# Attention into a gated MLP on one core: another order for the first loads, and a last output piece in two parts

## The chip, the cores and the metric

The kernel runs on one core of a Trainium2 chip. The metric is the device time of one execution in microseconds; the profile's span, from the first to the last instruction, lies inside it. The engines are named as in the profile: PE (TensorE matmul), PEld (its weight loads), DVE (VectorE), ACT (ScalarE), POOL (GpSimd) and SP (SyncE, which issues most DMAs).

## The reference

Eight batches, 12 heads, 448 positions, head size 64, all float32. An attention whose softmax has one extra term in its denominator feeds a layer with a mish-gated hidden width:

```python
scores = (q @ k.T) / sqrt(64)
m = max(scores, axis=-1)
e = exp(scores - m)
attn = e / (sum(e) + exp(-m) + 1e-9)
x = (attn @ v), heads side by side        # 3584 x 768
h = x @ w_in                              # 3584 x 2048
g = h * tanh(softplus(h))
out = g @ w_out                           # 3584 x 768, float32
```

## The kernel before, in words

Work is cut into pairs of heads: 48 pairs, six to a batch, numbered through as p. A pair's q, k and v are loaded by `load_pair` (L118) as tiles of 112 partitions, each with 4 neighbouring positions of both heads, one DMA of 224 KB each, issued by SP in program order. `cast_pair` (L155) turns them into bf16: on GpSimd, except pair 0, whose q goes to VectorE and whose k goes to ScalarE. `transpose_pair` (L171) turns q and k by eight PE transposes into PSUM; for pair 0 q and k have a PSUM tile each, for the following pairs both share one. `evac_qk` (L199) brings them back to SBUF, q scaled by 1/8; for pair 0 ScalarE takes q and VectorE takes k.

`scores` (L244) does the matmuls of one of four steps of a pair into one of three PSUM tiles (`sc_tiles`), and VectorE's negated row maximum (L285). `exps` (L291) is ScalarE's exponential with its row sum (L298). `normalise` issues a DMA transpose of the exponentials on SP (L370), or `turn_on_pe` does part of it on PE (L381); `spread_rden` spreads the reciprocals over PSUM by matmuls (L341); `av_pair` multiplies by v (L407). `mm1_mish` does the first MLP product (L438) and mish on ScalarE (L444). `mm2_part` (L463) is the second product (L485), cut into small chunks that fill PE between attention steps. Its `evac` copies PSUM to an output tile on VectorE (L472), and `store_rows` (L448) issues the stores on SP (L456), two DMAs for 128 rows, because the rows of one tile belong to two of the interleaved position sets; the very last tile (group 3, tile 6) is stored in two column parts as these are ready. For its last 128 rows the first DMA has 16 rows and the second 112.

The order is written out by hand: `tc.manual_schedule()` keeps each engine's instructions in program order, and semaphores are set by the tiles that instructions read and write. Buffers: 3 for each loaded float32 tile, 4 for the bf16 q and k, 12 for the bf16 v. In the built program a load is also held until the one eight places before it on SP has landed.

The program begins like this (L535 on): three pairs are loaded, each as q, k, v; pairs 0 and 1 are cast and transposed, with pair 0's evacuation and its first three score steps after its own transposes; then pair 3 is loaded, pair 2 cast, three weight pieces are issued on GpSimd's queue (`load_w`), pair 4 is loaded. Then the first batch's six pairs follow in a loop of pairs and steps (the head); evacuation of pair 1 follows the first `exps`. After that come units of three pairs with the MLP work between them.

Of the kernel before, what the change touches and what calls it, by code (L numbers as in the profile page):

```python
# [10 lines left out]
BF16 = mybir.dt.bfloat16  # L11
AF = mybir.ActivationFunctionType
ALU = mybir.AluOpType
AX = mybir.AxisListType

UNIT_PAIRS = 3
# [3 lines left out]
def kernel(  # L20
# [9 lines left out]
    nc = tc.nc  # L30

    B, H, S, D = q.shape
# [3 lines left out]
    NT = 4  # L36
    SP_ = S // NT
# [9 lines left out]
    SCALE = 1.0 / float(D) ** 0.5  # L47
# [5 lines left out]
    def pool(name, bufs, space=None):  # L53
# [18 lines left out]
    sc_tiles = [  # L72
        psum.tile([128, 2, 512], FP32, tag=f"sc{i}", name=f"sc{i}") for i in range(3)
    ]
# [26 lines left out]
    loaded, casted, qkT, att, xT, o_sbs, stats = {}, {}, {}, {}, {}, {}, {}  # L101
# [3 lines left out]
    def flush_late():  # L105
        while late:
            late.popleft()()

    def mo_take():

        if not mo_free:
            flush_late()
        return mo_free.popleft()
# [1 line left out]
    spread_copy = {}  # L115


    def load_pair(p):  # L118
        if p >= N_PAIRS:
            return  # L120
        b, h0 = p // HP, (p % HP) * 2
        tiles = []
        for nm, src in (("q", q), ("k", k), ("v", v)):
            t = ld_pool.tile([SP_, 2, NT * D], FP32, tag=f"{nm}_f", name=f"{nm}_f")
            nc.sync.dma_start(  # L125
                out=t, in_=src[b, h0 : h0 + 2].rearrange("h (p t) d -> p h (t d)", t=NT)
            )
            tiles.append(t)
        loaded[p] = tiles


    def w_pieces():
# [16 lines left out]
    def load_w(n):  # L149
        for _ in range(min(n, len(pieces))):  # L150
            dst, src = pieces.popleft()
            nc.gpsimd.dma_start(out=dst, in_=src.rearrange("(a p) c -> p a c", p=128))


    def cast_pair(p):  # L155
        if p >= N_PAIRS:
            return
        q_f, k_f, v_f = loaded.pop(p)
        q_bf = bf_pool.tile([SP_, NT, 2, D], BF16, tag="q_bf", name="q_bf")
        k_bf = bf_pool.tile([SP_, NT, 2, D], BF16, tag="k_bf", name="k_bf")  # L160
        v_bf = bf_pool.tile([SP_, 2, NT * D], BF16, tag="v_bf", name="v_bf", bufs=12)
        by_t = "p h (t d) -> p t h d"
        cast_q, cast_k = nc.gpsimd.tensor_copy, nc.gpsimd.tensor_copy
        if p == 0:
            cast_q, cast_k = nc.vector.tensor_copy, nc.scalar.copy
        cast_q(out=q_bf, in_=q_f.rearrange(by_t, t=NT))  # L166
        cast_k(out=k_bf, in_=k_f.rearrange(by_t, t=NT))  # L167
        nc.gpsimd.tensor_copy(out=v_bf, in_=v_f)  # L168
        casted[p] = (q_bf, k_bf, v_bf)

    def transpose_pair(p, bank=None):  # L171
        if p >= N_PAIRS:
            return
        q_bf, k_bf, _ = casted[p]
        if bank is None:
            ps = mo_take()
            ps_k = mo_take() if p == 0 else ps
        else:
            ps, ps_k = sc_tiles[2 - bank][:, 0, :], sc_tiles[2 - bank][:, 1, :]
        by_s = [  # L180
            t[:, :].bitcast(BF16).rearrange("p (s n) -> p s n", s=2)[:, s, :]
            for s, t in enumerate((ps, ps_k))
        ]
        for s, src in enumerate((q_bf, k_bf)):
            for t in range(NT):
                nc.tensor.transpose(  # L186
                    by_s[s][:, t * SP_ : (t + 1) * SP_],
                    src[:, t].rearrange("p h d -> p (h d)"),
                    ident[:SP_, :SP_],
                )  # L190
        own = [] if bank is not None else [ps, ps_k] if p == 0 else [ps]
        qkT[p] = (by_s, own)

    def apart(later, *earlier):

        for e in earlier:
            tc.declare_no_dep(later.ins, e.ins, reason="they read different PSUM banks")

    def evac_qk(p, act=False):  # L199
        if p >= N_PAIRS:  # L200
            return
        (q_ps, k_ps), own = qkT[p]
        mo_free.extend(own)
        q_reads = []
        qd = q_diag[p % 3]
        kT = qk_pool.tile([128, S], BF16, tag="kT", name="kT")
        if p < DIAG_FROM:
            qT = qd.rearrange("d i h r -> d (i h r)")[:, 0:S]
            qkT[p] = (qT, kT)
            if act:  # L210
                nc.scalar.mul(qT, q_ps[:, 0:S], SCALE)
            else:
                q_reads.append(nc.vector.tensor_scalar(
                    out=qT, in0=q_ps[:, 0:S], scalar1=SCALE, scalar2=None, op0=ALU.mult
                ))
        else:
            qkT[p] = (qd, kT)
            if p < DIAG_FROM + 3:
                nc.vector.memset(qd[0:64, :, 1, :], 0.0)
                nc.vector.memset(qd[64:128, :, 0, :], 0.0)  # L220
            for h in range(2):
                rows = slice(64 * h, 64 * h + 64)
                q_reads.append(nc.vector.tensor_scalar(  # L223
                    out=qd[rows, :, h, :],
                    in0=q_ps[rows, 0:S].rearrange("d (i r) -> d i r", i=QB),
                    scalar1=SCALE, scalar2=None, op0=ALU.mult,
                ))
        if p == 0 or own and not act:
            nc.vector.tensor_copy(out=kT, in_=k_ps[:, 0:S])
        else:  # L230
            k_read = nc.scalar.copy(kT, k_ps[:, 0:S])  # L231
            if not own:
                apart(k_read, *q_reads)
# [3 lines left out]
    def scores_ahead(limit):  # L237

        while rg["next"] < limit and rg["used"] < len(sc_tiles):
            rg["used"] += 1  # L240
            scores(rg["next"])
            rg["next"] += 1
# [202 lines left out]
        if not spare:  # L445
            mo_free.append(h_ps)

    def store_rows(g, i, o_sb, cols):  # L448

        r = i * 128  # L450
        while r < (i + 1) * 128:
            seg = r // SP_
            n = min((i + 1) * 128, (seg + 1) * SP_) - r
            b, t, c0 = 2 * g + seg // NT, seg % NT, r % SP_
            rows = out[b * S : (b + 1) * S, :].rearrange("(c t) m -> t c m", t=NT)
            nc.sync.dma_start(  # L456
                out=rows[t, c0 : c0 + n, cols], in_=o_sb[r - i * 128 : r - i * 128 + n, cols]
            )
            r += n
# [3 lines left out]
    def mm2_part(g, i, q0, nq):  # L463

        cols, n_cols = slice(q0 * NQ, (q0 + nq) * NQ), nq * NQ
        st = {}

        def evac():
            if (g, i) not in o_sbs:
                o_sbs[g, i] = [o_pool.tile([128, d_model], FP32, tag="o_sb", name="o_sb"), 0]  # L470
            o_sb, have = o_sbs[g, i]
            nc.vector.tensor_copy(out=o_sb[:, cols], in_=st["o"][:, 0:n_cols])  # L472
            mo_free.append(st["o"])
            o_sbs[g, i][1] = have + nq
            if (g, i) == (B // 2 - 1, 6):
                store_rows(g, i, o_sb, cols)
            elif have + nq == 4:
                store_rows(g, i, o_sb, slice(0, d_model))

        def chunk(f0, f1):  # L480
            if f0 == 0:
                flush_late()
                st["o"] = mo_take()
            for ff in range(f0, f1):
                nc.tensor.matmul(  # L485
                    st["o"][:, 0:n_cols],
                    lhsT=gT[:, ff, i * 128 : (i + 1) * 128],
                    rhs=w_out_sb[:, ff, cols],
                    start=(ff == 0), stop=(ff == FF_T - 1),
                )  # L490
            if f1 == FF_T:
                late.append(evac)

        step = 2
        return [(lambda f0=f0: chunk(f0, f0 + step), nq) for f0 in range(0, FF_T, step)]
# [36 lines left out]
    TURN_BY_ACT = {(HEAD - 1, 3)}  # L532

    W_AT = ({1: 1, 5: 1, 9: 1}, {1: 1, 5: 1, 7: 1, 9: 1, 11: 1}, {1: 1, 3: 1, 5: 1, 7: 1})
    for p in range(UNIT_PAIRS):  # L535
        load_pair(p)
    for p in range(2):
        cast_pair(p)
        transpose_pair(p)
        if p == 0:  # L540
            evac_qk(p, act=True)
            scores_ahead(3)
    load_pair(3)
    cast_pair(2)
    load_w(3)
    load_pair(4)


# [35 lines left out]
    for u in range(UNITS_PER_B, N_UNITS + 2 * UNITS_PER_B):  # L584
# [10 lines left out]
        for n in range(steps):  # L595
            pi, s = divmod(n, STEPS)
            p, idx = p0 + pi, p0 * STEPS + n
            late_tp = u == UNITS_PER_B and n == STEPS
            if late_tp:
                transpose_pair(p0 + 2)  # L600
# [38 lines left out]
        for f in range(FF_U):  # L639
# [19 lines left out]
            if f in (3, FF_U - 1) and p0 >= LATE_DIV:  # L659
                p = todo[1 + f // (FF_U - 1)]  # L660
# [33 lines left out]
```

## Time and profile before

| what | value |
|---|---|
| median of 3 runs | 493.13 us (493.05 to 497.79) |
| the profiled execution, device time | 488.69 us |
| its span | 486.9 us |
| mean granted TensorE clock | 0.987 |
| PE busy | 453.3 us, 93% of the span |
| VectorE busy | 359.4 us, 74% |
| ScalarE busy | 345.4 us, 71% |
| GpSimd busy | 103.4 us, 21% |
| HBM read, written | 45.61 MB, 11.01 MB |

How to read it: in the page's picture of 40 slices PE is at nine tenths or more from the eleventh slice on, save for the last one. The chain of waits follows the work that ended last, backwards. A timeline row has start, duration, engine, line, operation, output and input tile, and the idle time before it with what ended it. [...] The profiled execution was quicker than any of the three timed runs, so the steps of a sum are held against the execution, and only their difference is set against the median.

### The profile page before, as it was taken

The page shows a single profiled execution, that of the slowest core. Times are in us where ns is not written, and L with a number is a line of the kernel's source. Part 1 is how long each engine was busy: PE and PEld are TensorE (multiplying, and loading weights), DVE is VectorE, ACT ScalarE, POOL GpSimd, SP SyncE. Part 2 cuts the span into 40 slices and gives each one's busy share as a digit, 9 for nine tenths or more (in the row PEclk, how much of TensorE's full clock was granted, in tenths as well). Part 3 has the DMA queues.
Part 4 walks back from the last instruction along what each step waited for, and adds up shares of the span by engine and source line. Part 5 has one row for each costly group of instructions (what it writes and reads, how often), then busy time and mean ns, then how long its engine had stood idle before and what let it go on. Part 6 is the DMA issues. An engine that isn't in the chain of part 4 may idle for free.

```text
span 486.9 us, 9223 instructions
## 1 busy us (share of the span) xinstructions
PE 453.3 (93%) x3219; PEld 258.4 (53%) x3219; DVE 359.4 (74%) x713; ACT 345.4 (71%) x905; POOL 103.4 (21%) x184
## 2 busy tenths in 40 slices
PE   4676896898999999999999999999999999999996
PEld 2344454554655565555555555555555555556563
DVE  4889738758889898889899888889898978520011
ACT  5998859677687887879687868788797968412300
POOL 4534535206013030403012120404040200000000
PEclk9999798999999999999999999999999999999999
DMA  8999999999998979799999998998979886761122
GB/s 233 221 235 206 265 197 241 145 185 246 143 220 224 204 195 197 230 194 258 164 247 174 221 209 190 223 199 223 199 236 164 210 152 142 146 146 31 36 59 72
DMA packets 204975, 91.08 MB, mean 187 GB/s; under 512 B 161792, under 2 KB 201472, under 8 KB 204928
## 3 DMA queue, kind: packets, MB, share of 16 engines
q1 hardware_dynamic: 197440, 84.20, 79.5%
q0 software_dynamic: 7488, 6.29, 9.0%
q8 instruction: 25, 0.41, 0.4%
q14 instruction: 22, 0.18, 0.1%
HBM read 45.61 MB, written 11.01 MB: 116 GB/s over the span
## 4 chain that ended last, share of the span: by engine, by line
PE 75%; ACT 11%; DVE 8%; DMA 2%; issue 2%; SPq 1%; POOL 0%; DVEq 0%; ACTq 0%
PE mo L438 26%; PE mo L485 24%; ACT en L298 9%; PE sc L264 7%; DVE negm L285 6%; PE sc L407 5%; PE sc L438 4%; PE sc L186 3%; PE mo L407 2%; DMA k_f<-in_k_dram 1%; PE mo L341 1%; PE sc L270 1%; DMA v_f<-in_v_dram 1%; SPq L125 1%; DVE eT L385 1%
## 5 line engine op out<-in xcount | busy, mean ns | idle before, releaser
L298 ACT ACTIVATE en<-sc,negm 128x448 bf16<-128x448 f32 x336 | 208.4, 641 | 22.6 <-DVE negm L285 20.7
L285 DVE TENSOR_REDUCE negm<-sc 128x2 f32<-128x896 f32 x192 | 183.0, 971 | 44.8 <-PE sc L264 28.2
L485 PE MATMUL mo<-w_out_sb,gT 128*128 128x384 bf16 (+1 forms) x1024 | 166.7, 306 | 0.0
L438 PE MATMUL mo<-xT,w_in_sb 128*128 128x448 bf16 x672 | 141.9, 353 | 0.5 <-DVE xT L417 0.3
L485 PEld LDWEIGHTS <-gT 128*128 128x128 bf16 x1024 | 96.3, 98 | 55.4 <-issue 1.3
L444 ACT ACTIVATE gT<-mo 128x448 bf16<-128x448 f32 x112 | 59.6, 543 | 83.0 <-PE mo L438 82.7
L438 PEld LDWEIGHTS <-w_in_sb 128*128 128x128 bf16 x768 | 72.7, 98 | 63.6 <-issue 3.3
L166 POOL CAST q_bf<-q_f 112x512 bf16<-112x512 f32 x47 | 29.3, 623 | 230.8 <-DMA q_f<-in_q_dram 208.0
L362 DVE TENSOR_SCALAR en<-en,rden 128x448 bf16<-128x448 bf16 x252 | 73.6, 365 | 0.8
L264 PE MATMUL sc<-kT,qd 128*128 128x448 bf16 x252 | 71.6, 354 | 0.0
L298 ACT ACTIVATION_READ_ACCUMULATOR en<-sc,negm 128x1 f32 x336 | 71.1, 212 | 0.0
L472 DVE COPY o_sb<-mo 128x384 f32<-128x384 f32 (+1 forms) x64 | 32.1, 501 | 48.3 <-PE mo L485 48.1
L264 PEld LDWEIGHTS <-qd 128*128 128x128 bf16 x252 | 24.6, 97 | 28.8 <-issue 12.9
L407 PE MATMUL sc<-eT,v_bf 112*64 112x448 bf16 x288 | 34.1, 357 | 2.1 <-ACT en L298 1.6
L223 DVE TENSOR_SCALAR qd<-sc 64x448 bf16<-64x448 bf16 x72 | 27.7, 385 | 7.5 <-PE sc L186 6.6
L407 PEld LDWEIGHTS <-v_bf 112*64 112x64 bf16 x384 | 20.9, 111 | 22.3 <-issue 15.6
L168 POOL CAST v_bf<-v_f 112x512 bf16<-112x512 f32 x48 | 29.9, 624 | 12.2 <-DMA v_f<-in_v_dram 11.5
L167 POOL CAST k_bf<-k_f 112x512 bf16<-112x512 f32 x47 | 29.1, 619 | 9.1 <-DMA k_f<-in_k_dram 8.0
L270 PE MATMUL sc<-kT,qd 64*128 64x448 bf16 x36 | 15.8, 457 | 7.7 <-ACT en L298 7.2
L186 PEld LDWEIGHTS <-q_bf 112*128 112x128 bf16 x192 | 14.3, 103 | 15.4 <-DVE q_bf L166 4.2
L231 ACT COPY kT<-sc 128x448 bf16<-128x448 bf16 x39 | 20.8, 534 | 0.6 <-PE sc L186 0.6
L438 PE MATMUL sc<-xT,w_in_sb 128*128 128x448 bf16 x96 | 20.8, 353 | 0.0
(53 smaller groups left out, 279.2 us busy)
## 6 DMA issues: line engine op xcount, KB each, us to landing
q_f<-in_q_dram SPq DMA_DIRECT2D x48, 224.0 KB, 5.3
k_f<-in_k_dram SPq DMA_DIRECT2D x48, 224.0 KB, 5.4
v_f<-in_v_dram SPq DMA_DIRECT2D x48, 224.0 KB, 5.5
w_in_sb<-in_moe_w_in_dram POOLq DMA_DIRECT2D x12, 256.0 KB, 7.3
w_out_sb<-in_moe_w_out_dram POOLq DMA_DIRECT2D x8, 384.0 KB, 7.4
out_dram<-o_sb SPq DMA_DIRECT2D x7, 336.0 KB, 3.5
out_dram<-o_sb SPq DMA_DIRECT2D x8, 288.0 KB, 5.0
out_dram<-o_sb SPq DMA_DIRECT2D x8, 240.0 KB, 3.5
```

The costliest lines, as they stand in the source:

```text
L166: cast_q(out=q_bf, in_=q_f.rearrange(by_t, t=NT))
L167: cast_k(out=k_bf, in_=k_f.rearrange(by_t, t=NT))
L168: nc.gpsimd.tensor_copy(out=v_bf, in_=v_f)
L264: nc.tensor.matmul(sc[:, bk, 0:S], lhsT=qT[:, i].rearrange("d h r -> d (h r)"), rhs=kT, start=True, stop=True,)
L285: nc.vector.tensor_reduce(out=negm, in_=sc[:, 0 : len(cols), 0:S], axis=AX.X, op=ALU.max, negate=True)
L298: e = nc.scalar.activation(out=st["en"][:, :, c, 0:SP_], in_=sc[:, bk, 0:S].rearrange("q (j c) -> q j c", j=NT), func=AF.Exp, bias=st["neg ...
L362: nc.vector.tensor_scalar(out=en[:, :, i, 0:SP_], in0=en[:, :, i, 0:SP_], scalar1=st["rden"][:, i : i + 1], scalar2=None, op0=ALU.mult,)
L407: nc.tensor.matmul(av[h * 64 : (h + 1) * 64, 0:S], lhsT=v_bf[:, h, j * D : (j + 1) * D], rhs=e_h, start=(j == 0), stop=(j == NT - 1),)
L438: nc.tensor.matmul(h_ps[:, 0:S], lhsT=w_in_sb[:, dm, ff * 128 : (ff + 1) * 128], rhs=xT[b][:, dm, :], start=(dm == 0), stop=(dm == DM_T - 1),)
L444: nc.scalar.activation(out=gT[:, ff, b % 2 * S : b % 2 * S + S], in_=h_ps[:, 0:S], func=AF.Mish)
L472: nc.vector.tensor_copy(out=o_sb[:, cols], in_=st["o"][:, 0:n_cols])
L485: nc.tensor.matmul(st["o"][:, 0:n_cols], lhsT=gT[:, ff, i * 128 : (i + 1) * 128], rhs=w_out_sb[:, ff, cols], start=(ff == 0), stop=(ff == ...
```

## The change

What it does, in four pieces:

- The first nine loads stand in another order on SP: k 0, q 0, q 1, k 1, v 0, q 2, k 2, v 1, v 2.
- Pair 0 is cast on VectorE alone: k first, then q in two halves (two of the four column blocks each). PE turns k first, then q, with the second half of q going to a free score tile, `sc_tiles[2]`. ScalarE evacuates k, VectorE evacuates q in two halves.
- The casts of v for pairs 0, 1 and 2 are their own function on GpSimd: v 0 after the casts of q and k of pair 1, v 1 and v 2 after those of pair 2.
- In the very last output piece (384 columns) VectorE copies the first 192 columns and ScalarE the other 192; of its two stores the one of 16 rows is issued on ScalarE's queue, the one of 112 rows stays on SP.

```diff
-    def load_pair(p):
+    def load_pair(p, names="qkv"):
...
-        for nm, src in (("q", q), ("k", k), ("v", v)):
+        for nm in names:
+            src = dict(q=q, k=k, v=v)[nm]
...
-    def cast_pair(p):
+    def cast_pair(p, with_v=True):
...
         if p == 0:
-            cast_q, cast_k = nc.vector.tensor_copy, nc.scalar.copy
-        cast_q(out=q_bf, in_=q_f.rearrange(by_t, t=NT))
-        cast_k(out=k_bf, in_=k_f.rearrange(by_t, t=NT))
-        nc.gpsimd.tensor_copy(out=v_bf, in_=v_f)
+            nc.vector.tensor_copy(out=k_bf, in_=k_t)
+            for half in (slice(0, NT // 2), slice(NT // 2, NT)):
+                nc.vector.tensor_copy(out=q_bf[:, half], in_=q_t[:, half])
+        else:
+            nc.gpsimd.tensor_copy(out=q_bf, in_=q_t)
+            nc.gpsimd.tensor_copy(out=k_bf, in_=k_t)
         casted[p] = (q_bf, k_bf, v_bf)
+        if with_v:
+            cast_v(p)
+
+    def cast_v(p):
+        nc.gpsimd.tensor_copy(out=casted[p][2], in_=loaded.pop(p)["v"])
...
-        for s, src in enumerate((q_bf, k_bf)):
+        by_2 = sc_tiles[2][:, 0, :].bitcast(BF16)
+        srcs = list(enumerate((q_bf, k_bf)))
+        for s, src in reversed(srcs) if p == 0 else srcs:
             for t in range(NT):
+                to = by_2 if p == 0 and s == 0 and t >= NT // 2 else by_s[s]
                 nc.tensor.transpose(
-                    by_s[s][:, t * SP_ : (t + 1) * SP_],
+                    to[:, t * SP_ : (t + 1) * SP_],
...
+            if p == 0:
+                nc.scalar.copy(kT, k_ps[:, 0:S])
+                by_2 = sc_tiles[2][:, 0, :].bitcast(BF16)
+                for ps, half in (q_ps, slice(0, S // 2)), (by_2, slice(S // 2, S)):
+                    nc.vector.tensor_scalar(
+                        out=qT[:, half], in0=ps[:, half], scalar1=SCALE, scalar2=None,
+                        op0=ALU.mult,
+                    )
+                return
...
-            nc.sync.dma_start(
+            (queue if queue is not None and n < SP_ else nc.sync).dma_start(
...
-            nc.vector.tensor_copy(out=o_sb[:, cols], in_=st["o"][:, 0:n_cols])
+            last = (g, i, have + nq) == (B // 2 - 1, 6, 4)
+            n_dve = n_cols // 2 if last else n_cols
+            nc.vector.tensor_copy(
+                out=o_sb[:, cols.start : cols.start + n_dve], in_=st["o"][:, 0:n_dve]
+            )
+            if last:
+                nc.scalar.copy(o_sb[:, cols.start + n_dve : cols.stop], st["o"][:, n_dve:n_cols])
...
-                store_rows(g, i, o_sb, cols)
+                store_rows(g, i, o_sb, cols, queue=nc.scalar if last else None)
...
-    for p in range(UNIT_PAIRS):
-        load_pair(p)
+    for p, names in (0, "kq"), (1, "qk"), (0, "v"), (2, "qk"), (1, "v"), (2, "v"):
+        load_pair(p, names)
     for p in range(2):
-        cast_pair(p)
+        cast_pair(p, with_v=False)
         transpose_pair(p)
         if p == 0:
-            evac_qk(p, act=True)
+            evac_qk(p)
             scores_ahead(3)
     load_pair(3)
-    cast_pair(2)
+    cast_v(0)
+    cast_pair(2, with_v=False)
+    cast_v(1)
+    cast_v(2)
```

More of the change, by code (lines that the diff above doesn't have):

```diff
@@ L121, in load_pair @@
         b, h0 = p // HP, (p % HP) * 2
-        tiles = []
-        for nm, src in (("q", q), ("k", k), ("v", v)):
+        for nm in names:
+            src = dict(q=q, k=k, v=v)[nm]
             t = ld_pool.tile([SP_, 2, NT * D], FP32, tag=f"{nm}_f", name=f"{nm}_f")
@@ L127, in load_pair @@
             )
-            tiles.append(t)
-        loaded[p] = tiles
+            loaded.setdefault(p, {})[nm] = t
     def w_pieces():
@@ L152, in load_w @@
             nc.gpsimd.dma_start(out=dst, in_=src.rearrange("(a p) c -> p a c", p=128))
-    def cast_pair(p):
+    def cast_pair(p, with_v=True):
         if p >= N_PAIRS:
             return
-        q_f, k_f, v_f = loaded.pop(p)
+        q_f, k_f, v_f = (loaded[p].get(nm) for nm in "qkv")
         q_bf = bf_pool.tile([SP_, NT, 2, D], BF16, tag="q_bf", name="q_bf")
@@ L162, in cast_pair @@
         by_t = "p h (t d) -> p t h d"
-        cast_q, cast_k = nc.gpsimd.tensor_copy, nc.gpsimd.tensor_copy
+        q_t, k_t = (t.rearrange(by_t, t=NT) for t in (q_f, k_f))
         if p == 0:
-            cast_q, cast_k = nc.vector.tensor_copy, nc.scalar.copy
-        cast_q(out=q_bf, in_=q_f.rearrange(by_t, t=NT))
-        cast_k(out=k_bf, in_=k_f.rearrange(by_t, t=NT))
-        nc.gpsimd.tensor_copy(out=v_bf, in_=v_f)
+            nc.vector.tensor_copy(out=k_bf, in_=k_t)
[4 more added lines that the diff above has]
+            nc.gpsimd.tensor_copy(out=k_bf, in_=k_t)
         casted[p] = (q_bf, k_bf, v_bf)
+        if with_v:
+            cast_v(p)
+    def cast_v(p):
+        nc.gpsimd.tensor_copy(out=casted[p][2], in_=loaded.pop(p)["v"])
     def transpose_pair(p, bank=None):
@@ L227, in evac_qk @@
                 ))
-        if p == 0 or own and not act:
+        if own and not act:
             nc.vector.tensor_copy(out=kT, in_=k_ps[:, 0:S])
@@ L446, in mm1_mish, with store_rows @@
             mo_free.append(h_ps)
-    def store_rows(g, i, o_sb, cols):
+    def store_rows(g, i, o_sb, cols, queue=None):
         r = i * 128
```

## The prediction

> **What bounds the kernel now.** I read four views: the page's head, the chain of waits, the timeline of the first 16 us, and the last 5 us. First the page:
>
> ```profile
> span 486.9 us, 9223 instructions
> PE 453.3 (93%) x3219; PEld 258.4 (53%) x3219; DVE 359.4 (74%) x713; ACT 345.4 (71%) x905; POOL 103.4 (21%) x184
> PE 75%; ACT 11%; DVE 8%; DMA 2%; issue 2%; SPq 1%; POOL 0%; DVEq 0%; ACTq 0%
> ```
>
> TensorE (PE) carries three quarters of the chain. The change touches none of that steady part: compared in the built programs, every engine's order is the same outside the first and last dozen instructions. So the question is how much earlier the steady part begins, and how much sooner the span closes after PE's last matmul. The chain of waits, from the start (start us, us, what):
>
> ```profile
> 2.67 5.62 DMA k_f<-in_k_dram
> 8.35 0.62 POOL k_bf L167
> 9.02 0.57 PE mo L186 x4
> 9.61 0.54 ACT qd L211
> 10.58 2.47 ACT en L298 x8
> ```
>
> What ends last at the start is not the first pair but the second: its k load is the fifth transfer in the queue, then GpSimd casts it, PE turns it, and ScalarE (ACT) evacuates it between two exponentials. The timeline shows both pairs:
>
> ```profile
> 3.73 0.43 DVE L166 CAST q_bf<-q_f 112x512 bf16<-112x512 f32 x1 [1.67 <-DMA q_f<-in_q_dram]
> 4.22 0.55 PE L186 MATMUL mo<-ident,q_bf 112*128 112x112 bf16 x4 [4.22 <-DVE q_bf L166]
> 4.50 0.62 ACT L167 CAST k_bf<-k_f 112x512 bf16<-112x512 f32 x1 [2.48 <-DMA k_f<-in_k_dram]
> 5.17 0.56 PE L186 MATMUL mo<-ident,k_bf 112*128 112x112 bf16 x4 [0.40 <-ACT k_bf L167]
> 5.77 0.39 DVE L229 COPY kT<-mo 128x448 bf16<-128x448 bf16 x1 [1.61 <-PE mo L186]
> 6.21 0.53 PE L270 MATMUL sc<-kT,qd 64*128 64x448 bf16 x1 [0.48 <-DVE kT L229]
> 6.73 0.60 POOL L168 CAST v_bf<-v_f 112x512 bf16<-112x512 f32 x1 [5.43 <-DMA v_f<-in_v_dram]
> 6.80 3.09 DVE L285 TENSOR_REDUCE negm<-sc 128x2 f32<-128x896 f32 x3 [0.65 <-PE sc L273]
> 7.52 0.61 POOL L166 CAST q_bf<-q_f 112x512 bf16<-112x512 f32 x1 [0.18 <-DMA q_f<-in_q_dram]
> 7.93 0.63 ACT L298 ACTIVATE en<-sc,negm 128x448 bf16<-128x448 f32 x1 [2.37 <-DVE negm L285]
> 8.35 0.61 POOL L167 CAST k_bf<-k_f 112x512 bf16<-112x512 f32 x1 [0.22 <-DMA k_f<-in_k_dram]
> 9.15 0.61 POOL L168 CAST v_bf<-v_f 112x512 bf16<-112x512 f32 x1 [0.18 <-DMA v_f<-in_v_dram]
> 9.61 0.54 ACT L211 ACTIVATE qd<-mo 128x448 bf16<-128x448 bf16 x1 [0.34 <-PE mo L186]
> ```
>
> Each cast starts as its transfer lands, so the rows give landings by place in the queue: 3.7, 4.5, 6.7, 7.5, 8.3, 9.1 us. From the third place on, one place is worth 0.80 to 0.83 us. ACT's row at 9.61 has 0.34 us of idle before it: it had the first exponentials done at 9.27 and waited for pair 1's k.
>
> **Part 1, the head.** Pair 0: k takes the first place and its cast goes from ACT to VectorE (DVE): 3.73 + 0.43 = 4.16; PE turns k from 4.21 to 4.77; ACT's copy of kT, which DVE did in 0.39, I take from the 0.54 row of the same shape on ACT: done 5.35. q lands at 4.5; its cast in halves costs between 0.21 (half of 0.43) and 0.43 each; I take 0.25, nearest to half, so 4.75 and 5.0. PE turns two blocks (half of 0.55) after each: 5.08 and 5.33. DVE scales the first half by about 5.4 (a quarter of a us), PE's first scores start at 5.45 instead of 6.21 and the first reduce near 6.05 instead of 6.80. ACT's first exponential moves from 7.93 to 7.18, its pair is done at 8.52 instead of 9.27: 0.75 us earlier. With halves as dear as wholes (casts to 5.36, scale 0.39 to 5.78) the shift is only 0.38. The ACT queue loses a cast and an evacuation and gains one copy; nothing queued behind waits longer.
>
> Pair 1: q and k take places 3 and 4 instead of 4 and 5, k lands 0.83 us earlier, GpSimd casts it from 7.52, PE is done near 8.75, ACT evacuates at 8.78 instead of 9.61. That is later than 8.52, so the landing sets the shift: **-0.83 us**. From there ACT works without a gap in both versions and the next reduces and pair 2's transposes (place 7 instead of 8) move at least as far.
>
> The v loads: v of pair 0 goes from place 3 to 5, of pair 1 from 6 to 8, of pair 2 stays at 9. GpSimd's casts keep the same seven landing times, so its weight loads behind them stay where they are. The cover for v is large, the first product with v starts only here (PE, then the SP queue's transposes, below):
>
> ```profile
> 31.86 1.71 PE L407 MATMUL mo<-eT,v_bf 112*64 112x448 bf16 x8
> 58.35 0.95 PE L407 MATMUL mo<-eT,v_bf 112*64 112x448 bf16 x8
> ```
>
> If it were gone, v of pair 0 would cost its two places, 1.6 us. On SP, pair 3's v load now waits for the late cast of v 0 (free near 8.96; it was issued at 7.53) and pair 4's for v 1 (near 11.4 instead of 9.98), with the loads of pairs 4 and 5 behind them. Up to eight transfers of 0.8 us are queued ahead by then, so I cost it at nothing; without that cover it is 1.4 us.
>
> **Does the shift reach the steady part?** It would not, if loads or the transposes on SP bound the stretch to 60 us. SP is close to that:
>
> ```profile
> 14.55 8.74 SPq L370 DMA_TRANSPOSE eT<-en  x1
> 43.52 7.65 SPq L370 DMA_TRANSPOSE eT<-en  x1
> DMA to landing us min/median/max: 11.6/11.6/11.6
> ```
>
> The transpose at 14.55 stands behind the loads and its queue is free again only at 23.3; I expect that end to stay. The last row is the landing of the one at 43.52: 55.1, and PE uses it in the row at 58.35, 3.2 us later. That is the tightest of the five; 0.83 fits in. No PE row of the stretch waits for a transfer. So the whole shift is carried.
>
> **Part 2, the tail** (timeline; then the DVE row of a 192 wide copy, ACT's 448 wide one, ACT's shortest; then the SP group and the two landings):
>
> ```profile
> 482.70 0.56 DVE L472 COPY o_sb<-mo 128x384 f32<-128x384 f32 x1 [2.04 <-PE mo L485]
> 483.28 0.78 SPq L456 DMA_DIRECT2D out_dram<-o_sb  x2
> 472.30 0.36 DVE L472 COPY o_sb<-mo 128x192 f32<-128x192 f32 x1 [0.96 <-PE mo L485]
> 31.49 0.53 ACT L350 COPY rb<-mo 128x448 f32<-128x448 f32 x1 [0.35 <-PE mo L341]
> 8.46 0.19 ACT L298 ACTIVATION_READ_ACCUMULATOR en<-sc,negm 128x1 f32 x1
> out_dram<-o_sb SPq DMA_DIRECT2D x2, 168.0 KB, 2.2
> out_dram<-o_sb SPq DMA_DIRECT2D x2, 24.0 KB, 1.5
> ```
>
> Now: copy to 483.26, the 16-row store is issued, then the 112-row store at about 483.65, landing some 2.2 later. After: DVE copies 192 columns to 483.06, ACT the other 192. In the built program ACT's copy waits for VectorE's last increment, which is DVE's half, although they touch different columns: both read one PSUM tile. So the halves run one after the other. ACT's half lies between 0.19 and 0.53; by width I take 0.33: 483.43, and SP issues the 112-row store at about 483.46, because the 16-row one has gone to ACT's queue and, with 1.5 us to land, ends sooner. **-0.19 us**; bounds: 0 (ACT takes 0.53), and -0.57 if the halves did run side by side. [...]
>
> Sum: -0.83 - 0.19 = **-1.0 us**. The profiled execution took 488.69 (486.9 span and 1.8 around it), so its like would take 487.7. The median of the runs shown, 493.13, lies 4.4 above that execution; I apply the difference to it: **492.1 us**.
>
> **Rivals.** (a) The PE clock. One operation by window (us, PE busy with count, PEld, clock granted, DMA), then all engines' windows:
>
> ```profile
> 8.00:34.00 26.00, 6.34 (x12) 0.99 (x12) 1.00 1.17 234
> 34.50:48.00 13.50, 2.85 (x8) 0.73 (x8) 0.99 1.03 216
> 31.00:34.40 3.40, 3.40 (x27) 1.35 (x24) 2.19 (x3) 3.05 (x11) 0.00 (x0) 1.00 1.17 294
> 31.80:35.20 3.40, 3.13 (x22) 1.36 (x21) 2.16 (x6) 3.24 (x11) 0.01 (x1) 1.00 1.15 283
> 48.00:51.40 3.40, 3.40 (x26) 2.42 (x27) 3.31 (x6) 2.70 (x10) 2.48 (x4) 0.53 1.50 176
> 54.80:58.20 3.40, 3.40 (x30) 1.45 (x28) 2.42 (x3) 3.24 (x11) 2.40 (x4) 0.52 1.11 337
> 78.80:82.20 3.40, 3.40 (x27) 2.30 (x26) 3.40 (x5) 3.30 (x12) 2.17 (x3) 0.54 1.16 189
> ```
>
> The scores matmul took 0.53 us before 34 and 0.36 after, and three windows of 3.4 us ran at half clock; that PE work would need 3.4 x 0.36 / 0.53 = 2.3, so a slow window costs up to 1.1 us. The change moves work by 0.83 us against these windows: what fell in 31.8 to 35.2, less dense, now falls in the one before PE sped up. If PE speeds up two windows later, this costs 2.2: **494.3, slower than before**; one window, 1.1, already eats the gain. Against it: most of that stretch waits on ACT and DVE. (b) The same the other way, one to three slow windows fewer: 491.0 to 488.8. [...] (c) The shift is swallowed by loads and SP's queue before 60 us; only the tail stays: **492.9**. For it: SP's row at 14.55; against it: the 3.2 us. (d) The gap between the second and third landing, 2.2 us instead of 0.8, falls on k or q of pair 0: their chain is 1.4 late, its exponentials end near 9.9 instead of 9.27, the head is 0.3 later: 493.2. If it belongs to v instead, k of pair 1 lands two places after 4.5, near 6.1, and the exponentials' end at 8.52 sets the shift, 1.1: 491.8.
>
> **How the numbers follow.** Forecast with its own range, 491.5 to 492.8 (head -1.1 to -0.38, tail -0.57 to 0): 0.5. (a) with one window or two, 0.15; (b) 0.18; (c) 0.12; (d) late 0.05. The range goes from two slow windows fewer (492.1 - 2.2 = 489.9) to two more (494.3), a little wider at both ends since the three runs shown span 4.7 us: 489.5 to 494.8. Faster, same and slower are cut at 1% (4.9 us), about what a measurement of this kernel can tell from no change. Faster than 488.2 needs more than three windows: 0.06; slower than 498.1: 0.05; within: 0.89.
>
> **What would show it.** Right: the first reduce near 6.05, the first exponential near 7.2, ACT's evacuation of pair 1 near 8.8 with a short idle before it, PE's first matmuls of L438 (the mixture layer) 0.8 earlier if the slow windows are equal, ACT's last copy beginning after DVE's, end of span some 4.0 after PE's last matmul instead of 4.2. Wrong: pair 1's k cast still at 8.3, a PE wait on a transfer or on eT between 20 and 60 us, or the two last copies side by side.

## The result and the profile after

The changed kernel took 490.05 us, the median of 12 executions (488.07 to 499.21), against 493.94 us for the kernel before in the same comparison (12 executions, 491.22 to 497.79). The ratio is 0.9935, with a 95% interval of 0.9908 to 0.9962; here and below it is worked out over fast executions alone (without the slow one of 499.21), and is not the quotient of the two medians, 0.9921. The forecast, 492.1 against 493.13, was a ratio of 0.9979. So the result lies within 1%, as forecast, and inside the range; but the interval leaves the forecast out. By that interval the gain is 1.9 to 4.5 us, not 1.0.

The two profiles alone would have said the opposite. The page of the changed kernel:

```profile
span 487.8 us, 9225 instructions
PE 454.1 (93%) x3219; PEld 258.1 (53%) x3219; DVE 361.8 (74%) x716; ACT 345.1 (71%) x905; POOL 103.7 (21%) x184
PE 72%; ACT 11%; DVE 9%; DMA 5%; issue 2%; SPq 0%; DVEq 0%; ACTq 0%
```

Its span is 0.9 us longer than the one before, 486.9, because the profiled execution of the kernel before (488.69 us) was quicker than all 12 of its executions here. What the reader is to see is the last line: DMA has 5% of the chain instead of 2%. That comes from one wait in mid-kernel, told below.

The start, in the timeline of the changed kernel (start us, length us, engine, line, operation, idle before it and what ended it):

```profile
3.83 0.43 DVE L164 CAST k_bf<-k_f 112x512 bf16<-112x512 f32 x1 [1.76 <-DMA k_f<-in_k_dram]
4.71 0.50 DVE L166 CAST q_bf<-q_f 112x256 bf16<-112x256 f32 x2 [0.46 <-DMA q_f<-in_q_dram]
4.90 0.53 ACT L220 COPY kT<-mo 128x448 bf16<-128x448 bf16 x1 [2.88 <-PE mo L195]
5.47 0.28 DVE L223 TENSOR_SCALAR qd<-mo 128x224 bf16<-128x224 bf16 x1 [0.26 <-PE mo L195]
6.40 3.83 DVE L303 TENSOR_REDUCE negm<-sc 128x2 f32<-128x896 f32 x4 [0.45 <-PE sc L291]
6.88 0.61 POOL L169 CAST k_bf<-k_f 112x512 bf16<-112x512 f32 x1 [0.52 <-DMA k_f<-in_k_dram]
7.53 0.63 ACT L316 ACTIVATE en<-sc,negm 128x448 bf16<-128x448 f32 x1 [2.10 <-DVE negm L303]
8.76 0.54 ACT L229 ACTIVATE qd<-mo 128x448 bf16<-128x448 bf16 x1
```

The order is the one foretold, and so are the lengths: two half casts in 0.50, a half scaled in 0.28. The last row is the one to compare: ScalarE's evacuation of pair 1 begins at 8.76 instead of 9.61. It has no idle time before it. The k of pair 1 landed at 6.88, 1.47 earlier, and the exponentials of pair 0 end last, not the landing.

The end, in the timelines of the changed kernel (the last rows, and the SP row of the last store):

```profile
483.16 0.36 DVE L492 COPY o_sb<-mo 128x192 f32<-128x192 f32 x1 [2.04 <-PE mo L509]
483.56 0.32 ACT L496 COPY o_sb<-mo 128x192 f32<-128x192 f32 x1 [20.63 <-DMA out_dram<-o_sb]
483.90 0.39 ACTq L474 DMA_DIRECT2D out_dram<-o_sb  x1
483.90 0.32 SPq L474 DMA_DIRECT2D out_dram<-o_sb  x1
```

The copies run one after the other, 0.04 apart. Both stores leave at 483.90. The landings of these two, in the DMA view (KB, us to landing):

```profile
out_dram<-o_sb SPq DMA_DIRECT2D x1, 168.0 KB, 2.2
out_dram<-o_sb ACTq DMA_DIRECT2D x1, 24.0 KB, 2.4
```

The small store now lands last, at 486.3. On SP's queue it took 1.5.

### The profile page after: what moved, and what is told of

Its sections match the earlier page's. It is cut to its first block, busy times and chain, and to the rows that moved or that the text cites. A ratio compares the mean times of both kernels' runs of the same rounds, so it can differ in the third digit from the quotient of the medians.

```text
span 487.8 us, 9225 instructions
## 1 busy us (share of the span) xinstructions
PE 454.1 (93%) x3219; PEld 258.1 (53%) x3219; DVE 361.8 (74%) x716; ACT 345.1 (71%) x905; POOL 103.7 (21%) x184
## 4 chain that ended last, share of the span: by engine, by line
PE 72%; ACT 11%; DVE 9%; DMA 5%; issue 2%; SPq 0%; DVEq 0%; ACTq 0%
PE mo L456 25%; PE mo L509 23%; ACT en L316 9%; PE sc L282 7%; DVE negm L303 6%; PE sc L425 6%; DMA eT<-en 4%; PE sc L456 3%; PE sc L195 3%; PE mo L425 2%; DVE eT L403 1%; PE sc L288 1%; PE mo L359 1%; DMA q_f<-in_q_dram 1%; DVE xT L435 0%
## 5 line engine op out<-in xcount | busy, mean ns | idle before, releaser
L462 ACT ACTIVATE gT<-mo 128x448 bf16<-128x448 f32 x112 | 59.6, 543 | 83.3 <-PE mo L456 83.0
L380 DVE TENSOR_SCALAR en<-en,rden 128x448 bf16<-128x448 bf16 x252 | 76.0, 373 | 0.8
L435 DVE CAST xT<-sc 128x448 bf16<-128x448 f32 x33 | 20.3, 615 | 0.0
```

The lines of the kernel that those rows point to most:

```text
L380: nc.vector.tensor_scalar(out=en[:, :, i, 0:SP_], in0=en[:, :, i, 0:SP_], scalar1=st["rden"][:, i : i + 1], scalar2=None, op0=ALU.mult,)
L462: nc.scalar.activation(out=gT[:, ff, b % 2 * S : b % 2 * S + S], in_=h_ps[:, 0:S], func=AF.Mish)
```

## The experiments

Three accounts stood against each other. The forecast: the head is 0.8 to 1.1 earlier, the tail 0.2, everything between is carried. The clock: an earlier head also makes PE speed up earlier, and that is the surplus. The draw: the head gives what was forecast, and the rest is scatter between executions.

### One part at a time

The first four ran on one chip beside 35 executions of the kernel before (median 492.17). The first is the kernel before, unchanged.

> The kernel before against itself. If the 3.9 us between the two medians (493.94 and 490.05) belong to the change, this shows no difference: a ratio of 1.000 with an interval of about 0.003 either way. If they came from the draw of executions, the two copies differ by 1 us or more too. Its trace is also a second look at the kernel before: the one in hand (488.69) was quicker than all twelve timed executions, and a usual one should show 3 to 5 us more of waiting somewhere between 14 and 480 us.

Measured: 492.16 us (489.72 to 494.79), ratio 1.0003 (0.9976 to 1.0031). The comparison is level to 0.3%. Its profiled span was 490.5, 3.6 longer than that of the same program above.

The head alone is the changed kernel with

```diff
-            last = (g, i, have + nq) == (B // 2 - 1, 6, 4)
+            last = False
```

> The head of the change alone: order of loads, pair 0 on VectorE, the later casts of v; the last output piece as before. By the prediction's sum it is 0.83 us faster than before. The rival: the head is worth far more than its 0.83 us because an earlier start also spares waits for transfers later; then it keeps nearly all of the 3.9 us, a ratio near 0.992.

Measured: 490.37 us (487.86 to 495.92), ratio 0.9937 (0.9907 to 0.9967). By the ratio the whole gain, 3.1 us, is here; the two medians alone are 1.8 us apart.

The tail alone is the kernel before with the changed `store_rows` and `evac`:

```diff
+            last = (g, i, have + nq) == (B // 2 - 1, 6, 4)
+            n_dve = n_cols // 2 if last else n_cols
...
+                nc.scalar.copy(o_sb[:, cols.start + n_dve : cols.stop], st["o"][:, n_dve:n_cols])
...
+                store_rows(g, i, o_sb, cols, queue=nc.scalar if last else None)
```

> The last output piece of the change alone, the head as before. Prediction: 0.19 us faster. From the profile after, where the span ended 4.66 us after the last matmul instead of 4.22: 0.4 us slower. In no theory more than 0.6 us either way, so a ratio between 0.999 and 1.001; a larger gain would put the surplus into the tail.

Measured: 492.30 us (491.49 to 505.02), ratio 0.9999 (0.9980 to 1.0019). No gain shows, but the interval is 0.9 us wide to either side, too coarse for a term of 0.19. Its landings, in the DMA view of the tail-only kernel:

```profile
out_dram<-o_sb SPq DMA_DIRECT2D x1, 168.0 KB, 2.3
out_dram<-o_sb ACTq DMA_DIRECT2D x1, 24.0 KB, 2.5
```

The small store is slow on ScalarE's queue here too. In both kernels with the new tail it leaves at the same moment as the large one, where it went 0.37 ahead of it before; so the queue and the overlap with the large store are not told apart.

Pair 0's part alone keeps q, k, v of each pair together:

```diff
-    for p, names in (0, "kq"), (1, "qk"), (0, "v"), (2, "qk"), (1, "v"), (2, "v"):
+    for p, names in (0, "kqv"), (1, "qkv"), (2, "qkv"):
...
-        cast_pair(p, with_v=False)
+        cast_pair(p)
```

and the casts of v stand where they were; the tail is as before.

> Of the head only pair 0's part: k before q, both on VectorE, q in halves, ScalarE's copy of k; v 0 stays in the third place and q, k of pair 1 in the fourth and fifth, v casts in their old places; tail as before. By the prediction nothing is gained: the first exponentials are about 0.5 us earlier, but ScalarE then waits for pair 1's k, whose evacuation stays near 9.6 us. If the 3.9 us come from pair 0's part (its copies leaving ScalarE, or PE's order), this keeps them, a ratio near 0.992.

Measured: 491.65 us (488.01 to 495.46), ratio 0.9988 (0.9960 to 1.0017). Its timeline on ScalarE:

```profile
7.19 0.64 ACT L316 ACTIVATE en<-sc,negm 128x448 bf16<-128x448 f32 x1 [1.90 <-DVE negm L303]
9.60 0.54 ACT L229 ACTIVATE qd<-mo 128x448 bf16<-128x448 bf16 x1 [1.07 <-PE mo L195]
```

The first exponential is earlier, 7.19 instead of 7.93, and the second pair's evacuation is where it was, 9.60, after 1.07 of idle. In this trace pair 0's gain is lost in the wait for pair 1's k, and pair 3's reciprocal comes at 34.93, where it was (34.92). So it is the reordered loads that pass it on; they were not run alone.

### The head cut out

To lift the head out of the noise, both kernels were cut after the first unit. The cut leaves out everything behind it: the other units, the normalisation of the last unit, all but the first six weight pieces, and all stores but one small one of zeros.

```diff
+    LAST = UNITS_PER_B + 1
-    for u in range(UNITS_PER_B, N_UNITS + 2 * UNITS_PER_B):
+    for u in range(UNITS_PER_B, LAST):
```

> The kernel before, cut off after the first eight groups of the first MLP product (near 73 us in its trace). It leaves out all later units, the weight pieces and transposes that only serve those, and nearly all of the output. It is to be held against the same cut of the kernel after, execution by execution. If the whole surplus of the change arises in the first 60 us from the PE clock (traces in hand: first MLP matmul at 59.5 to 61.3 us where PE sped up at 34 us, at 63.7 to 64.4 where it stayed slow to 53 us), these executions lie in two groups some 3 us apart, most of them in the slow one.

> The kernel after, cut in the same place and leaving out the same work. Prediction: every execution is 0.8 us shorter, so the median too (near 1.1% of 75 us). If the change also makes PE speed up early more often, the median is about 3 us shorter, with the two groups in place and the fast one fuller. If the surplus comes from transfers after 60 us, 0.8 us here.

Measured: before 80.34 us (79.26 to 82.26), after 77.73 (77.53 to 78.28). The difference is 2.6, more than the forecast's head. A longer cut, after the third unit, keeps all weight pieces and leaves out the later units and the normalisation of its last one, its transposes with it (the expectation speaks of these as kept):

```diff
+    LAST = UNITS_PER_B + 3
```

> The kernel before, cut off after the MLP groups of the fifth unit (near 131 us in its trace), past the stretch in which one profile of the kernel after waited 2.2 us for a transposed tile. It leaves out all later units, the transposes of the last unit kept, and nearly all of the output. To be held against the same cut of the kernel after. If its executions spread by 4 us or more, the spread of the whole kernel arises before 131 us.

> The kernel after, cut in the same place and leaving out the same work. Prediction: 0.8 us shorter. If transfers between 60 and 125 us give the surplus, 2 to 3 us shorter here while the shorter cut shows 0.8. If the PE clock gives it, 2 to 3 us in both cuts. If the head start is given back in waits for transposed tiles, less than 0.8 us here.

Measured: before 140.71 (137.83 to 141.02), after 141.23 (137.47 to 150.16). With such a spread it says nothing on sizes.

The next two keep the short cut and issue the score matmuls of pairs 2 to 5 twice in the first three of a pair's four steps, so that PE is denser in the stretch in which it speeds up. That it then speeds up early in every execution was the author's guess. If the surplus was the clock, the two kernels should then differ by the shift of the head alone. The unfilled cuts ran again beside them, all four on another chip than the first cuts.

```diff
+            for _ in range(2 if 2 <= p < HP else 1):
```

> The short cut of the kernel before, with the score matmuls of pairs 2 to 5 issued twice in the first three steps (same operands, same place, so nothing else changes). It leaves out what the short cut leaves out. If the PE clock is what the surplus hangs on, PE now speeds up by about 35 us in every execution and stays fast to 60: no execution near 81 to 82, the median at or below the fast ones of the plain cut (79.3). If the clock has nothing to do with it, the extra matmuls cost time or nothing, and the spread of 3 us stays.

> The short cut of the kernel after with the same matmuls twice, leaving out what the short cut leaves out. Clock theory: PE sped up in time here already, so little changes (77.7 or somewhat less), and the distance to the same kernel before shrinks from 2.6 us to the head start alone, 0.8 to 1.0. Rival, the order of loads itself gives 2.6 us through transfers: the distance stays at 2.6.

> The short cut of the kernel before once more, on the same chip as the other three, leaving out what it left out; the first time 79.3 to 82.3 us, median 80.3. Clock theory: executions again spread over some 3 us, and the trace has pair 4's reciprocal 5.3 us after pair 3's if PE sped up by 36 us, 7 us after it if not.

> The short cut of the kernel after once more, leaving out what it left out; the first time 77.5 to 78.3 us in all executions. [...] If the first five executions were luck, some now lie 2 us higher and the medians come to within about 1 us.

Measured: filled, 79.08 before (78.06 to 79.93) and 77.31 after (76.51 to 80.02); not filled, 79.70 before (78.40 to 80.31) and 78.96 after (77.19 to 80.69). The tight set of the first cut did not come again: it was partly luck. Over both rounds the short cut has a mean of 80.03 before (12 executions) and 78.38 after (11): 1.6 less, with a standard error of 0.46. The two rounds differ much: 2.7 in the first, 0.7 in the second, on the other chip. Filled, the difference of the means is 1.4, with an error of 0.58. The fill did what it was to do, as far as the two traces tell: PE's clock rose by 32 us in both (at 31.99 before and 30.27 after), and pair 5's reciprocal came 10.54 and 10.47 after pair 3's (10.28 to 10.53 in the traces with an early rise, below). Against the unfilled cuts of the same chip the means are 0.5 lower before and 1.2 lower after, though work was added; the two kernels came no closer. The fill was meant to decide, and it did not.

### What the traces say of the clock

One row of the windows view for PE's score matmuls, 36 to 46 us (length, PE busy with count, PEld, granted clock, DMA). The kernel before, as profiled for the prediction:

```profile
36.00:46.00 10.00, 1.80 (x5) 0.55 (x6) 1.00 0.98 191
```

The same program a second time (the unchanged kernel of the experiments):

```profile
36.00:46.00 10.00, 2.76 (x5) 0.51 (x5) 0.50 1.01 208
23.00:53.00 30.00, 26.23 (x185) 14.45 (x185) 24.85 (x40) 25.07 (x78) 12.44 (x28) 0.50 1.11 196
```

The changed kernel:

```profile
36.00:46.00 10.00, 1.78 (x5) 0.46 (x5) 1.00 1.05 210
```

One program, two clocks: 0.36 us a matmul in one execution, 0.55 in the next, and 30 us without a break at half clock (the last row but one holds all engines: PE, PEld, DVE, ACT, POOL). The granted clock in these rows can't be read alone, though. The second run of the short cut of the kernel before has

```profile
36.00:46.00 10.00, 2.59 (x5) 0.41 (x4) 1.00 0.91 203
```

with 1.00 at 0.52 us a matmul, and so have three more of the five traces with long matmuls. The clock records of a trace begin with a rise (in the kernel before at 34.16, in the changed one at 34.54), and the view counts 1.00 ahead of it; so it does in the prediction's row for 8 to 34 us, 1.00 at 0.53. There the length of the matmul tells the speed. What a late rise costs is read from VectorE's reciprocals, one to a pair (here of pairs 0, 3 and 5). Kernel before, first execution:

```profile
17.32 0.20 DVE L318 RECIPROCAL rden<-den 128x7 f32<-128x7 f32 x1
34.92 0.20 DVE L318 RECIPROCAL rden<-den 128x7 f32<-128x7 f32 x1
45.21 0.20 DVE L318 RECIPROCAL rden<-den 128x7 f32<-128x7 f32 x1
```

Kernel before, second:

```profile
17.08 0.20 DVE L318 RECIPROCAL rden<-den 128x7 f32<-128x7 f32 x1
34.69 0.20 DVE L318 RECIPROCAL rden<-den 128x7 f32<-128x7 f32 x1
47.28 0.20 DVE L318 RECIPROCAL rden<-den 128x7 f32<-128x7 f32 x1
```

Changed kernel:

```profile
16.47 0.20 DVE L336 RECIPROCAL rden<-den 128x7 f32<-128x7 f32 x1
34.06 0.20 DVE L336 RECIPROCAL rden<-den 128x7 f32<-128x7 f32 x1
44.37 0.20 DVE L336 RECIPROCAL rden<-den 128x7 f32<-128x7 f32 x1
```

From pair 0 to pair 3 all take 17.6. From pair 3 to pair 5 it is 10.3 with PE at full clock and 12.6 without. All traces without fill (us; the matmul is the mean of the five in the 36 to 46 window, one at its edge counted with the part inside; the clock's rise is the first to full from 30 us on, from the clock records of the trace):

| kernel | ACT evacuates pair 1 | reciprocal of pair 3 | from there to pair 5 | a score matmul | clock rises |
|---|---|---|---|---|---|
| before | 9.61 | 34.92 | 10.29 | 0.36 | 34.16 |
| before, again | 9.36 | 34.69 | 12.59 | 0.55 | 53.20 |
| tail only (old head) | 9.79 | 35.12 | 12.61 | 0.48 | 53.41 |
| short cut, before | 9.86 | 35.19 | 10.53 | 0.36 | 35.16 |
| short cut, before, again | 8.91 | 34.24 | 12.63 | 0.52 | 52.43 |
| long cut, before | 9.36 | 34.69 | 12.28 | 0.47 | 42.49 |
| pair 0 only | 9.60 | 34.93 | 12.26 | 0.55 | 54.01 |
| after | 8.76 | 34.06 | 10.31 | 0.36 | 34.54 |
| head only | 8.40 | 33.73 | 10.29 | 0.36 | 34.06 |
| short cut, after | 8.90 | 34.22 | 10.29 | 0.36 | 33.68 |
| short cut, after, again | 8.45 | 33.78 | 10.28 | 0.36 | 33.18 |
| long cut, after | 8.46 | 33.79 | 10.30 | 0.36 | 34.40 |

The second and third columns move together: what ScalarE gains at pair 1 arrives unchanged at pair 3. Over the six traces with the old head and the five with the new the means are 9.48 and 8.59, and 34.81 and 33.92: 0.89 earlier. The fourth column is another matter: 2.0 to 2.3 us, which the new head saved in five traces of five and the old start of pair 1 in two of seven. By the first MLP matmul it has grown: 25.8 to 26.9 after pair 3's reciprocal in the seven traces that sped up early, 28.6 to 29.7 in the other five, 2.6 more on average. With equal odds for both, a split that far falls in 21 of the 792 ways to place seven early speed-ups among twelve traces, about one in 38.

From the rise at 34 us to 85 us the clock records of the two profiles differ too. In the kernel before the clock was at half from 47.82 to 51.23, from 54.64 to 58.05 and from 78.54 to 81.95, three stretches of 3.41 and 10.2 us in all; in the changed kernel from 51.61 to 58.43 and from 75.50 to 82.33, two of 6.83 and 13.7 us in all.

Why the clock rose at 34 us in one execution and at 53 in another was not shown. The new head moves the stretch ahead of pair 3's reciprocal and changes nothing else in it that these rows show: from pair 0's reciprocal to pair 3's it is 17.59 to 17.61 in all twelve traces, with either head. So five of five against two of seven may be luck, or the new head may make an early rise more frequent; twelve traces can't tell.

## Why the prediction was right or wrong

**Pair 0's chain: right.** The first reduce began at 6.40 in the profiled execution and at 6.04 to 6.54 in the five with the new head; 6.05 was forecast. The half casts cost about what half a cast costs: two in 0.50, a whole one 0.43.

**The head shift, -0.83: right in size, wrong in what sets it.** It was 0.85 in the pair of profiles and 0.89 on average. But pair 1's k came more than a place earlier, and the exponentials' end set the shift, which the second half of rival (d) had as the condition for 1.1. With the old head, too, ScalarE had no idle time before pair 1 in three of the six traces (9.36, 9.36 and 8.91): the landing set its start only in the other three. The single trace behind the forecast had its long gap between the second and third landing; over the traces the k of pair 1 landed anywhere from 7.46 to 8.60 in the old order and from 6.83 to 7.08 in the new one (without the filled cuts). A landing read from one execution is one draw.

**The loads of v and SP's queue at nothing: right up to 60 us.** In the changed kernel SP's first transpose row runs

```profile
13.70 9.54 SPq L388 DMA_TRANSPOSE eT<-en  x1
```

to 23.24, the end that was foretold, and no row of PE before 60 us waits for a tile that SP's transposes write. The first MLP matmul began at 60.59 instead of 61.30, 0.71 earlier with the clock alike in both.

**"So the whole shift is carried": failed behind 60 us, in some executions.** The tightest wait was looked for only up to there. The waits view of the changed kernel, 60 to 125 us, and of the head alone:

```profile
PE sc L425 <- DMA eT<-en: 2.2, 1, 2.2
```

```profile
PE sc L425 <- DMA eT<-en: 3.2, 1, 3.2
```

The same wait in the changed kernel's chain, and SP's rows there:

```profile
88.27 19.64 DMA eT<-en
107.95 0.95 PE sc L425 x8
```

```profile
59.77 12.04 SPq L388 DMA_TRANSPOSE eT<-en  x1
88.27 24.89 SPq L388 DMA_TRANSPOSE eT<-en  x3
```

The kernel before, SP's rows:

```profile
60.74 5.53 SPq L370 DMA_TRANSPOSE eT<-en  x1
88.64 18.91 SPq L370 DMA_TRANSPOSE eT<-en  x3
```

A head start moves PE up against these three transposes; where they take 25 to 27 us instead of 19 to 20, PE waits and the start is given back. From the first MLP matmul to that of the third unit the kernel before took 59.2 and 59.6 in its two executions, the changed one 60.8, the head alone 63.7. In these two the third unit starts at 121.3 and 123.2, later than the 120.5 of the kernel before with the same early rise of the clock: more than the whole shift is gone. The wait is not bound to the new head: the tail alone, with the old one, has it with 0.5 (27.0 for the transposes, 61.2 to the third unit), while the long cut of the kernel before had 24.4 and no wait. What makes the transposes slow in one execution and not in another was not tried.

**The tail, -0.19: failed at one step.** The copies ran in sequence, as the built program said, and the large store left 0.74 after VectorE's copy began, instead of 0.95: 0.21 sooner. The step that fell is "the 16-row one has gone to ACT's queue and, with 1.5 us to land, ends sooner": it took 2.4 and 2.5 there and lands last. From the start of VectorE's last copy to the last landing the old tail took 3.1 to 3.2 us (four kernels), the new one 3.1 and 3.3: what the issue gained, the landing lost. From the start of VectorE's last copy to the end of the span the old tail took 4.1 to 4.5 us (four kernels), the new one 4.3 and 4.6. The saved issue is seen here, 0.21, and so is the 0.9 to 1.0 that the small store took longer to land; whether its queue or the large store beside it cost that stays open.

**The slow windows taken as equal, and the surplus: the cause stays open.** The sum left the clock out, and the forecast's own range, 491.5 to 492.8, does not hold the measured 490.05; the wider range does, because it was drawn for rivals (a) and (b). Rival (b), the clock earlier, 0.18, had the measured level with 492.1 - 2.2 = 489.9 for two windows: 493.13 times 0.9935 is 489.9. That it had the cause is not shown. What a late rise of the clock costs is shown, 2.6 by the first MLP matmul; what makes it late is not. Nor were the slow windows equal: up to 82 us, behind the first rise, 10.2 us at half clock in the profile before and 13.7 in the one after. An estimate, if the shares of the twelve traces were the odds: 0.89 for the head, and 2.6 times the five in seven in which the clock rose late with the old start, 1.9, make 2.7, inside the 1.9 to 4.5 that were measured. But no run shows that the head changes the odds, and equal odds leave 0.89. The range held because it left room for the clock, and no run shows the clock as the cause; so far it was luck.

**What stays open.** That the gain lies in the head is shown by the ratios (head alone 0.9937, tail alone 0.9999, pair 0 alone 0.9988); that a late rise of the clock costs 2 us and more is shown by the traces. What decides on it, and that the change makes it rarer, is not shown; the 1 us or more that was gained beyond 0.89, by the ratio, has no shown cause. The rival recorded for the head alone, that an earlier start spares waits for transfers later, finds no support: both full traces with the new head waited more there, 2.2 and 3.2 us. The fill should have closed the gap to 0.9 and left 1.4, with an error of 0.6 that allows both. No version was run that beats both kernels; the 16-row store left on SP, with the copy in halves, was not tried.

## What to carry to other kernels

A change of a fifth of a per cent can't be read from one profile of each side: here the draw of the clock alone was worth more than 2 us, and the quicker kernel had the longer span. Repeat the profile of the unchanged program first, and see which of its numbers stay. Hold the granted clock against the length of one matmul before you believe it. And before you say that a change brings an event more often, ask which run shows that: here five of five against two of seven was one in 38 by equal odds, and no run had the cause. When a start is made earlier, follow the slack of every later transfer to the end of the start's influence, not to the first steady stretch; and when a small store is moved to another queue, ask for its landing there, not only for the issue time that it frees.

## What the hardware showed that was not expected

- The clock of one program rose at 34.16 us in one execution and was at half from 23 to 53 in another, with the same work.
- The view's granted clock reads 1.00 ahead of the first rise, with score matmuls of 0.53 us instead of 0.36.
- The first loads don't land at fixed places: k of pair 1 came between 7.46 and 8.60 us in the same order of loads.
- A 24 KB store of 16 rows took 1.5 us to land on SP's queue, 0.37 ahead of the large store, and 2.4 to 2.5 on ScalarE's, at the same moment as it.
- Three DMA transposes in a row held SP for 18.9 to 27.0 us between executions, and PE waited only in some of these.
